# Retention followed by two feed-forward blocks: all eight pairs of the first product of token chunks 2 and 3 by Strassen's scheme

## The chip, the core and the metric

The kernel runs on one core of a Trainium2 chip. Its engines are TensorE (PE in the profile; its weight loads have a row of their own, PEld), VectorE (DVE), ScalarE (ACT), GpSimd (POOL) and SyncE (SP), which here only issues DMAs. The metric is the device time of one execution in microseconds (us), as the median of several runs. The profile describes one execution.

## What is computed

```python
# retention: q, k, v of (2, 8, 768, 64); gamma and scale per head
for t in range(S):
    state = gamma * state + einsum('bhd,bhe->bhde', k[:, :, t], v[:, :, t])
    y[:, :, t] = scale * einsum('bhd,bhde->bhe', q[:, :, t], state)
x = y as (1536 tokens, 512)
# block 1: w_in (512, 2048), w_out (2048, 512)
h = x @ w_in
x = softplus(h) @ w_out
# block 2: w_in (512, 2048), w_out (2048, 512)
h = x @ w_in
out = (h * clip(h + 3, 0, 6) / 6) @ w_out
```

Some inputs arrive as float64, and the kernel makes float32 words of them itself (`Words.made`: raw bits to `cv` on ACT and DVE).

## The kernel before

**Arithmetic.** Every float32 operand of a product is split in two parts, high and low, each of which TensorE takes in one pass. A product is three passes: high x high, high x low, low x high. The split is always the same two instructions (`parted`): ACT copies the operand into the high part, DVE subtracts that from the operand for the low part.

**Tiles.** The 1536 tokens are three chunks of 512 columns (chunk 0, 1, 2 in the code; the words of the change call them 1, 2, 3). The hidden 2048 columns are 16 tiles f of 128. G1(c, f) is the first product of block 1 for one chunk and one tile: 12 matmuls of 128x512 into one bank. G2(c, f) is the second product: 12 matmuls of 128x512 into four accumulating banks. In between stands the softplus of one tile (`softplus`): DVE e, ACT e, DVE g, ACT hi, DVE lo.

**Strassen's scheme.** Two neighbouring tiles f are a pair p, eight in all. For chunks 1 and 2 together, a pair's first product is a 2x2 by 2x2 block product (two halves of the 512 input rows, two tiles, two chunks), and the scheme with seven half-products in place of eight makes it. The half-products are L1 to L7 (P1 to P7 in `early_step`), each 6 matmuls of 128x512. Seven of them give both tiles for both chunks, which plain G1 makes in 8 times 6 matmuls. The tokens' operands of the half-products are the tiles `xl`, one for each of the seven; four of them need sums that `early_operands` makes in place in the chunks' tiles `x` (t1 to t4). The weights' operands (`we`) come from the words of `w_in`, which are written to DRAM once (`words_in`), fetched again a pair at a time (`wf`) and summed by DVE (`sums`) in `early_in` and `forms`. The banks of a pair are combined in `early_step`: ACT `basel` copies L1's bank, L2 adds to that bank and ACT copies it to `g`; DVE then makes `partl`, `totall`, two `hs` and a `g`. Chunk 1's results go on as `g`; chunk 2's (`hs`) go to DRAM (`stash_h`) and come back later.

**Which pairs.** `PLAIN = 1`: pair 7 (tiles 14 and 15) is made by plain G1 for chunks 1 and 2, pairs 0 to 6 by the scheme.

**Order.** A planner (`Plan.run`) fixes each engine's order when the program is built: every task has an engine, a cost, what it waits for and a due time. The due times come from the list `pe`, which writes TensorE's order out: retention's blocks (`Tk`, `Tq`, `SS`, `DD`, `II`, `CC` for two blocks of 128 tokens at a time) stand in the gaps between the G1 and G2 of chunk 0, then come the half-products with G2 of chunk 1 between them (`behind`), then G2 of chunk 2, then block 2. Every engine runs its list in order; a waiting instruction holds up all behind it.

**What stays where.** A tile of weights has one of 20 slots `w`. The `w_out` tiles 8 to 15 are written to DRAM (`parts_out`) after chunk 0 and read back for chunks 1 and 2, except those of pair 7, which stay for chunk 1.

Of the kernel before, what the change touches and what calls it, by code (L numbers as in the profile page):

```python
# [18 lines left out]
P = 128  # L19
# [126 lines left out]
def kernel(ctx, tc, q, k, v, w1_in, w1_out, w2_in, w2_out, table, out):  # L146
# [19 lines left out]
    PLAIN = 1  # L166
# [80 lines left out]
    for name, n, shape, dtype in (("sums", 1, [P, 4, CH // 2], F32), ("wf", 1, [P, 2, CH], F32), ("xl", 7, [P, 2, 2, CH], F32R), ("hs", 3, [P, CH], F32), ("g2", 5, [P, CH], F32), ("hi2", 7, [P, CH], F32R), ("lo2", 7, [P, CH], F32R),  # L247
                                  ("basel", 1, [P, CH], F32), ("partl", 2, [P, CH], F32), ("totall", 1, [P, CH], F32), ("xf", 7, [P, 2, 2, QT], F32R), ("keep", START + 2, [P, CH], F32), ("tf0", 2, [P, 2, QT], F32), ("tf1", 2, [P, 2, QT], F32), ("tf2", 2, [P, 2, QT], F32),
# [25 lines left out]
    ORDER[2] = [f for pair in zip(range(KEPT), range(KEPT, NF)) for f in pair]  # L274
    FIRSTS = [c * NF + f for c in range(NC) for f in ORDER[min(c, 1)][:2 * PLAIN if c else NF]]
# [21 lines left out]
    for i, s in enumerate(FIRSTS):  # L297
        if s == 2 * NF + ORDER[1][0]:
            pe += [x for n in sorted(gaps) for x in gaps[n]] + [("L1", 0), ("L2", 0)]
            gaps.clear()  # L300
        for key in [("G1", s)] + ([("G2", FIRSTS[i - LAG])] if i >= LAG and FIRSTS[i - LAG] < 2 * NF else []):
# [5 lines left out]
    behind = [("G2", s) for s in FIRSTS[-LAG:] if s < 2 * NF]  # L307
# [30 lines left out]
    def dve(n):  # L338
        return (n + 151) / 960 - 0.05
# [65 lines left out]
    def weight(o, f, number):  # L405
# [28 lines left out]
        if not o and f // 2 in PAIRS:  # L434
            home = homes["in", f] = kept(f"words_in{f}", CH)
            T["S", key] = nc.add("SP", 0.45, lambda: nc.sync.dma_start(out=home, in_=x.w().bitcast(F32)), [t5], use, give=[x.cv_k] + made, load=0.8)
        elif o and f >= KEPT:
# [3 lines left out]
            for c_of in range(1 + (f in ORDER[1][:2 * PLAIN]), 3):  # L441
# [38 lines left out]
    def early_in(p):  # L480
        at = due["L1", p] - (12 if p else 18.0)
# [19 lines left out]
    def forms(m, p, words_of, t, words_k, at):  # L501
# [26 lines left out]
        for n, (source, cols, after, give) in enumerate((  # L528
# [3 lines left out]
                (lambda: pair(2), whole, [s3, s4], [sums[1]]))):  # L532
# [702 lines left out]
```

## Time and profile before

| | |
|---|---|
| time, median of 3 runs | 564.74 us (564.32 to 564.96) |
| the profiled execution's own time | 564.72 us |
| its span in the profile | 562.8 us |
| PE busy, 3685 matmuls | 553.3 us, 98% of the span |
| DVE, ACT busy | 440.5 us (78%), 367.1 us (65%) |
| from 150 us to 300 us: DVE busy by stretches of 50 us | 41.8, 44.4, 49.4 us |

The span runs from the first to the last instruction; the own time of the execution adds 1.9 us around it. Retention and chunk 0 fill the first 150 us, the half-products of chunks 1 and 2 with the G2 of chunk 1 the time to about 260 us, G2 of chunk 2 the time to some 300 us, block 2 the rest.

### The profile page before, as it was taken

To read this page: it belongs to the slowest core of one execution; us is meant where nothing else is said; L and a number is where in the kernel's file an instruction comes from. 1 tells how busy PE (TensorE), PEld (TensorE's weight loads), DVE (VectorE), ACT (ScalarE), POOL (GpSimd) and SP (SyncE) were. 2 spreads that over 40 slices of the span, in tenths; PEclk is the share of its full clock that TensorE was granted. 3 is DMA by queue.
4 is the path that set the end of the run, shared out by engine and by line. 5 is a ranking of instruction groups with operands and counts; after the bars stand their busy time and mean duration, and the time that the engine had idled before them with its cause. 6 is when DMAs were issued, how large, how long until landed. Compare 5 with 4: busy or idle time off the path is not lost.

```text
span 562.8 us, 9577 instructions
## 1 busy us (share of the span) xinstructions
PE 553.3 (98%) x3685; PEld 473.3 (84%) x3685; DVE 440.5 (78%) x778; ACT 367.1 (65%) x600; POOL 5.8 (1%) x13
## 2 busy tenths in 40 slices
PE   8899999999999999999999999999999999999996
PEld 6687788888788888888888999988998889988895
DVE  5999998889799778999998775837887897854443
ACT  4697999997774536687968734448778775432220
POOL 0000000000000000000000000000000000000000
PEclk9999999999999999999999999999999999999999
DMA  9997999994422216988907522243755752236003
GB/s 208 286 238 257 285 294 285 324 236 158 151 75 76 75 62 205 323 305 281 358 21 279 187 75 76 82 180 112 229 183 186 272 177 76 75 106 231 1 0 113
DMA packets 80829, 100.51 MB, mean 179 GB/s; under 512 B 41360, under 2 KB 58000, under 8 KB 80784
## 3 DMA queue, kind: packets, MB, share of 16 engines
q1 hardware_dynamic: 79776, 98.45, 54.3%
q0 software_dynamic: 720, 1.31, 1.3%
q8 instruction: 29, 0.48, 0.3%
q10 hardware_dynamic: 288, 0.14, 0.1%
q14 instruction: 16, 0.13, 0.1%
HBM read 74.98 MB, written 23.59 MB: 175 GB/s over the span
## 4 chain that ended last, share of the span: by engine, by line
PE 82%; DVE 5%; ACT 5%; DMA 5%; issue 1%; DVEq 0%; ACTq 0%; SPq 0%
PE banks L45 82%; DMA raw<-in_moe_w_in_dram 3%; ACT cv L45 2%; DMA raw<-in_moe_w_out_dram 1%; DVE g L45 1%; DVE cv L45 1%; DVE raw L45 1%; DVE lo L45 1%; DMA stash_out<-raw 1%; ACT hi L45 1%; ACT raw L45 0%; DVE qT L45 0%; DMA out_dram<-ob 0%; ACT between L45 0%; ACT w L45 0%
## 5 line engine op out<-in xcount | busy, mean ns | idle before, releaser
L45 PE MATMUL banks<-w,parts 128*128 128x512 f32 x579 | 136.7, 390 | 0.0
L45 PEld LDWEIGHTS banks<-w,parts 128*128 128x128 f32 x579 | 108.0, 188 | 21.3
L45 PE MATMUL banks<-hi,w 128*128 128x512 f32 x384 | 124.8, 393 | 0.0
L45 PE MATMUL banks<-xf,w 128*128 128x384 f32 x672 | 123.2, 337 | 0.4 <-DVE c L45 0.4
L45 PEld LDWEIGHTS banks<-xf,w 128*128 128x128 f32 x672 | 118.3, 188 | 3.4 <-DVE c L45 0.7
L45 PEld LDWEIGHTS banks<-hi,w 128*128 128x128 f32 x384 | 72.1, 188 | 15.0
L45 PE MATMUL banks<-xl,w 128*128 128x512 f32 x342 | 81.0, 391 | 0.2
L45 PEld LDWEIGHTS banks<-xl,w 128*128 128x128 f32 x342 | 63.7, 188 | 14.1 <-DVE hs L45 0.5
L45 PE MATMUL banks<-lo,w 128*128 128x512 f32 x192 | 75.1, 391 | 0.2 <-DVE lo L45 0.2
L45 ACT ACTIVATE e<-c,three 128x384 f32<-128x384 f32 (+1 forms) x32 | 24.6, 770 | 47.0 <-DVE c L45 46.5
L45 ACT ACTIVATE cv<-raw,half 128x512 uint32<-128x512 uint32 x64 | 48.6, 761 | 7.5 <-DMA raw<-in_moe_w_out_dram 3.7
L45 ACT ACTIVATE cv<-raw 128x512 f16<-128x512 int32 x64 | 50.0, 788 | 1.2
L45 DVE SCALAR_TENSOR_TENSOR cv<-raw,cv 128x512 uint32<-128x512 uint32 x64 | 44.1, 690 | 1.4
L45 PE MATMUL banks<-x_hi,w 128*128 128x512 f32 x128 | 42.5, 399 | 1.0 <-ACT x_hi L45 1.0
L45 PEld LDWEIGHTS banks<-lo,w 128*128 128x128 f32 x192 | 36.1, 188 | 7.9 <-DVE lo L45 0.9
L45 DVE TENSOR_SCALAR raw<-raw 128x512 f32<-128x512 f32 x76 | 32.3, 430 | 11.4 <-ACT raw L45 10.5
L45 ACT ACTIVATE hi<-g 128x512 fp32r<-128x512 f32 x48 | 29.9, 626 | 16.7 <-PE banks L45 10.1
L45 DVE TENSOR_TENSOR lo<-g,hi 128x512 fp32r<-128x512 f32 x48 | 33.0, 688 | 8.0 <-ACT hi L45 7.8
L45 ACT ACTIVATE parts<-c 128x768 fp32r<-128x768 f32 x32 | 26.9, 842 | 18.6 <-DVE c L45 18.6
L45 DVE TENSOR_TENSOR parts<-c,parts 128x768 fp32r<-128x768 f32 x32 | 30.6, 957 | 10.2 <-ACT parts L45 9.9
L45 ACT ACTIVATE e<-e 128x512 f32<-128x512 f32 x48 | 29.7, 624 | 9.3 <-DVE e L45 9.2
L45 ACT ACTIVATE raw<-raw 128x512 f32<-128x512 f32 x52 | 34.4, 668 | 0.7
(95 smaller groups left out, 653.5 us busy)
## 6 DMA issues: line engine op xcount, KB each, us to landing
raw<-in_moe_w_in_dram SPq DMA_DIRECT2D x32, 512.0 KB, 5.6
raw<-in_moe_w_out_dram SPq DMA_DIRECT2D x32, 512.0 KB, 5.7
w<-stash_out SPq DMA_DIRECT2D x32, 512.0 KB, 5.4
stash_out<-raw SPq DMA_DIRECT2D x16, 512.0 KB, 3.4
w<-parts_out SPq DMA_DIRECT2D x14, 512.0 KB, 5.4
parts_out<-w SPq DMA_DIRECT2D x8, 512.0 KB, 4.3
stash_h<-hs SPq DMA_DIRECT2D x16, 256.0 KB, 2.3
g<-stash_h SPq DMA_DIRECT2D x16, 256.0 KB, 4.6
```

The source lines that it names most:

```text
L45: return self.plan.tc.keep_in_program_order(getattr(self.engine, op)(*args, **kwargs))
```

## The change

Pair 7 is made by the scheme as well, so that `gemm1` is left with chunk 0 alone. The pairs come in the order 7, 6, 5, 4 (`LEADS`), then 0, 1, 2, 3 (`REST`). L1 and L2 of the four leads need no sums and no words from DRAM: they take the even tile's own parts (`("w", (0, 0, 2 * p))`) and chunk 1's tokens, and they stand where the plain G1 of pair 7 stood, in the gaps beside retention's last blocks. Since that holds four copies of L1's bank at once, `basel` has 4 slots. The operands `xl` and the sums in `x` are made in two halves of 256 tokens, so that the first half of chunk 2 can be worked on before its last two blocks are there. The `w_out` tiles 8 to 15 all stay for chunk 1 (`STAY`).

```diff
-    PLAIN = 1
+    FRONT = 4
...
-("basel", 1, [P, CH], F32)
+("basel", 4, [P, CH], F32)
...
-    PAIRS = range(NPAIR - PLAIN)
-    ORDER = [list(range(NF)) if c == 0 else list(range(2 * len(PAIRS), NF)) + list(range(2 * len(PAIRS))) for c in range(NC)]
+    PAIRS = [*reversed(range(NPAIR - FRONT, NPAIR)), *range(NPAIR - FRONT)]
+    LEADS, REST = PAIRS[:FRONT], PAIRS[FRONT:]
+    STAY = [2 * p + i for p in LEADS[:FRONT] for i in range(2)]
...
-    FIRSTS = [c * NF + f for c in range(NC) for f in ORDER[min(c, 1)][:2 * PLAIN if c else NF]]
+    FIRSTS = list(range(NF))
...
+    behind = [("G2", s) for s in FIRSTS[-LAG:]] + [("G2", NF + f) for f in ORDER[1][:2 * FRONT]]
+    for i, p in enumerate(LEADS):
+        for block in [("L1", p), ("L2", p)], behind[:1]:
+            pe += gaps.pop(n, [])
+            n += 1
+            pe += block
+        behind = behind[1:]
...
     for p in PAIRS:
-        if behind and p == 0:
-            pe += [("L1", p), behind[0], ("L2", p), behind[1]] + [(name, p) for name in ("L6", "L7", "L5", "L4", "L3")]
-        else:
-            pe += [(name, p) for name in (("L1", "L6", "L2", "L7") if p else ("L6", "L7"))] + behind[:1] + [(name, p) for name in ("L5", "L4", "L3")] + behind[1:]
-        behind = [("G2", NF + 2 * p + i) for i in range(2)]
+        pe += [(name, p) for name in (("L6", "L7") if p in LEADS else ("L1", "L6", "L2", "L7"))] + behind[:1] + [(name, p) for name in ("L5", "L4", "L3")]
+        behind = behind[1:]
+        if p in REST:
+            if p != REST[0]:
+                pe += behind[:1]
+                behind = behind[1:]
+            behind += [("G2", NF + 2 * p + i) for i in range(2)]
...
+            if n == 0 and not m and p in LEADS:
+                continue
...
     def early_operands():
...
+        n = CH // 2
+        for y in range(2):
+            cols = slice(y * n, (y + 1) * n)
+            have = [[t for u in range(c * START + 2 * y, c * START + 2 * y + 2) for t in ready["x", u]] for c in (1, 2)]
...
+            w_key, x_key = ("w", (0, 0, 2 * p)) if n == 0 and p in LEADS else ("we", p, n), ("xl", name)
```

Three places in the built order carry the prediction. Names in the rows: `xl` are the seven token operands, `w` a slot of weights, `hi` and `lo` the parts of a G2, `qT`, `kT` and `st` are retention's.

**TensorE, the leads' L1 and L2.** Before, plain G1 of pair 7 for chunk 1 (two operands `xl` in a row are one G1) stands ahead of retention's scores and its `vs,k` block, rows 407 to 423 of PE:

```order
L45 MATMUL banks<-xl_1664,w_1536 128x512 x6
L45 MATMUL banks<-xl_1668,w_1536 128x512 x6
L45 MATMUL banks<-qT_0_161,kT_0_159 64x64 x16
L45 MATMUL banks<-qT_1_162,kT_1_160 64x64 x16
```

Of the change, L1 and L2 of the leads in the same place and just behind it, rows 407 to 427 (lead 7 is `w_1540`, lead 6 `w_1336`; the rows of a G2 between are left out):

```order
L45 MATMUL banks<-xl_1641,w_1540 128x512 x6
L45 MATMUL banks<-qT_0_163,kT_0_161 64x64 x16
L45 MATMUL banks<-qT_1_164,kT_1_162 64x64 x16
L45 MATMUL banks<-xl_1644,w_1540 128x512 x6
...
L45 MATMUL banks<-xl_1641,w_1336 128x512 x6
L45 MATMUL banks<-hi_95,w_1551 128x512
L45 MATMUL banks<-lo_96,w_1551 128x512
L45 MATMUL banks<-hi_95,w_1551 128x512
L45 MATMUL banks<-xl_1644,w_1336 128x512 x6
```

L1 and L2 of a lead now have something between them: retention's scores for lead 7, three matmuls of a G2 for lead 6; retention's last `CC` stands there for lead 5, a whole G2 for lead 4.

**TensorE, the rest of the leads.** Rows 501 to 514 of the change, behind L6, L7 of lead 7 and a G2. In this order they are L5, L4, L3 of lead 7, then L6, L7, L5 of lead 6, L6 of lead 5, L4, L3 of lead 6, and L7, L5, L4, L3 of lead 5, of which the last eight rows stand here:

```order
L45 MATMUL banks<-xl_1788,w_1574 128x512 x6
L45 MATMUL banks<-xl_1852,w_1336 128x512 x6
L45 MATMUL banks<-xl_1925,w_1342 128x512 x6
L45 MATMUL banks<-xl_1766,w_79 128x512 x6
L45 MATMUL banks<-xl_1793,w_1540 128x512 x6
L45 MATMUL banks<-xl_1788,w_1336 128x512 x6
L45 MATMUL banks<-xl_1925,w_1381 128x512 x6
L45 MATMUL banks<-xl_1766,w_1540 128x512 x6
L45 MATMUL banks<-hi_94,w_81 128x512
```

Thirteen half-products follow each other here without a G2 between them. Before, the longest run without one is plain G1 of chunk 2 (four times 6 matmuls) and nine half-products, rows 487 to 499.

**VectorE, the operands behind retention's end.** From the first sum that needs chunk 2's last blocks to the low part of L6's operand, before (rows 237 to 245) and of the change (rows 245 to 256):

```order
L45 TENSOR_TENSOR x_183<-x_184,x_183 128x1024
L45 TENSOR_TENSOR xl_1943<-x_184,xl_1943 128x1024
L45 TENSOR_TENSOR xl_1958<-x_184,xl_1958 128x1024
L45 TENSOR_TENSOR x_184<-x_184 128x1024
L45 TENSOR_TENSOR x_184<-x_184,x_183 128x1024
L45 TENSOR_TENSOR sums_1760<-wf_1638 128x256 x2
L45 TENSOR_TENSOR sums_1760<-sums_1760,wf_1638 128x256
L45 TENSOR_TENSOR sums_1760<-wf_1638,sums_1760 128x256
L45 TENSOR_TENSOR xl_1982<-x_184,xl_1982 128x1024
```

```order
L45 TENSOR_TENSOR x_185<-x_186,x_185 128x2x256
L45 TENSOR_TENSOR x_186<-x_186 128x2x256
L45 TENSOR_TENSOR w_87<-sums_1850,w_87 128x512
L45 TENSOR_TENSOR sums_1850<-wf_1757 128x256 x2
L45 TENSOR_TENSOR sums_1850<-sums_1850,wf_1757 128x256
L45 TENSOR_TENSOR sums_1850<-wf_1757,sums_1850 128x256
L45 TENSOR_TENSOR lo_98<-g_93,hi_95 128x512
L45 TENSOR_TENSOR xl_1766<-x_186,xl_1766 128x2x256
L45 TENSOR_TENSOR x_186<-x_186,x_185 128x2x256
L45 TENSOR_TENSOR w_1342<-wf_1757,w_1342 128x256
L45 TENSOR_SCALAR e_90<-g_91 128x512
L45 TENSOR_TENSOR xl_1852<-x_186,xl_1852 128x2x256
```

The operations on tokens are half as long, and the first halves (not shown) stand ahead of these rows. Whole program: PE has 6 matmuls with `xl` fewer (336 for 342), SP 6 reads `w<-parts_out` of 512 KB fewer and 2 more writes of `words_in` and 2 more reads `wf`.

## Rows read from the trace of the kernel before

**Rows 1.** The page's first part: span, busy time and share of each engine.

```profile
span 562.8 us, 9577 instructions
PE 553.3 (98%) x3685; PEld 473.3 (84%) x3685; DVE 440.5 (78%) x778; ACT 367.1 (65%) x600; POOL 5.8 (1%) x13
```

**Rows 2.** Waits of PE from 27 us on: what for, total, times, longest.

```profile
PE banks L45 <- DVE c L45: 0.4, 1, 0.4
PE banks L45 <- DVE lo L45: 0.2, 1, 0.2
```

**Rows 3.** Windows: length, PE (matmuls), PEld, DVE, ACT, POOL, PE clock, DMA, GB/s.

```profile
132.00:140.00 8.00, 8.00 (x139) 6.39 (x137) 7.68 (x16) 5.84 (x11) 0.00 (x0) 1.00 0.43 151
140.00:150.00 10.00, 9.94 (x165) 7.85 (x162) 6.61 (x14) 5.80 (x11) 0.00 (x0) 1.00 0.62 211
170.00:180.00 10.00, 10.00 (x46) 8.28 (x45) 9.76 (x20) 4.79 (x10) 0.00 (x0) 1.00 0.08 28
180.00:190.00 10.00, 10.00 (x46) 8.29 (x45) 6.72 (x13) 4.36 (x8) 0.00 (x0) 1.00 0.31 105
250.00:260.00 10.00, 9.91 (x44) 7.88 (x43) 10.00 (x19) 5.65 (x10) 0.00 (x0) 1.00 1.00 362
```

**Rows 4.** Timeline of PE, 243 to 257 us: start, length, operation, count.

```profile
243.73 5.63 PE L45 MATMUL banks<-xl,w 128*128 128x512 f32 x24
249.20 0.39 PE L45 MATMUL banks<-hi,w 128*128 128x512 f32 x1
251.92 4.62 PE L45 MATMUL banks<-xl,w 128*128 128x512 f32 x18
256.38 0.39 PE L45 MATMUL banks<-hi,w 128*128 128x512 f32 x1
```

**Rows 5.** Timeline of all engines around the first pair's L1 and L2.

```profile
147.33 1.66 PE L45 MATMUL banks<-xl,w 128*128 128x512 f32 x6
148.92 0.69 PE L45 MATMUL banks<-qT,st 64*64 64x64 f32 x32
149.03 0.60 ACT L45 ACTIVATE basel<-banks 128x512 f32<-128x512 f32 x1
149.68 1.66 PE L45 MATMUL banks<-xl,w 128*128 128x512 f32 x6
149.68 1.09 ACT L45 ACTIVATE x<-banks 128x512 f32<-128x512 f32 x2
150.80 1.23 DVE L45 TENSOR_TENSOR x<-x,x 128x1024 f32<-128x1024 f32 x1 [1.02 <-ACT x L45]
151.17 0.39 PE L45 MATMUL banks<-hi,w 128*128 128x512 f32 x1
```

**Rows 6.** Timeline of PE, retention's scores at 135 us.

```profile
134.97 1.16 PE L45 MATMUL banks<-qT,kT 64*64 64x64 f32 x64
136.07 0.50 PE L45 MATMUL banks<-hi,w 128*128 128x512 f32 x1
```

**Rows 7.** Timeline of DVE, two stretches.

```profile
127.92 2.36 DVE L45 TENSOR_TENSOR xl<-x,xl 128x1024 fp32r<-128x1024 f32 x2
130.19 0.69 DVE L45 TENSOR_TENSOR w<-cv,w 128x512 fp32r<-128x512 f32 x1
...
251.42 0.68 DVE L45 TENSOR_TENSOR totall<-partl,banks 128x512 f32<-128x512 f32 x1
252.02 0.42 DVE L45 TENSOR_SCALAR e<-g 128x512 uint32<-128x512 uint32 x1
252.35 0.68 DVE L45 TENSOR_TENSOR lo<-g,hi 128x512 fp32r<-128x512 f32 x1
...
254.16 0.68 DVE L45 TENSOR_TENSOR hs<-totall,banks 128x512 f32<-128x512 f32 x1
```

**Rows 8.** The page's sixth part: DMA issues, KB each, median us to landing.

```profile
stash_h<-hs SPq DMA_DIRECT2D x16, 256.0 KB, 2.3
wf<-words_in SPq DMA_DIRECT2D x14, 256.0 KB, 3.0
```

More of the change, by code (lines that the diff above doesn't have):

```diff
@@ L247 @@
     for name, n, shape, dtype in (("sums", 1, [P, 4, CH // 2], F32), ("wf", 1, [P, 2, CH], F32), ("xl", 7, [P, 2, 2, CH], F32R), ("hs", 3, [P, CH], F32), ("g2", 5, [P, CH], F32), ("hi2", 7, [P, CH], F32R), ("lo2", 7, [P, CH], F32R),
-                                  ("basel", 1, [P, CH], F32), ("partl", 2, [P, CH], F32), ("totall", 1, [P, CH], F32), ("xf", 7, [P, 2, 2, QT], F32R), ("keep", START + 2, [P, CH], F32), ("tf0", 2, [P, 2, QT], F32), ("tf1", 2, [P, 2, QT], F32), ("tf2", 2, [P, 2, QT], F32),
+                                  ("basel", 4, [P, CH], F32), ("partl", 2, [P, CH], F32), ("totall", 1, [P, CH], F32), ("xf", 7, [P, 2, 2, QT], F32R), ("keep", START + 2, [P, CH], F32), ("tf0", 2, [P, 2, QT], F32), ("tf1", 2, [P, 2, QT], F32), ("tf2", 2, [P, 2, QT], F32),
                                   ("base", 1, [P, QT], F32), ("part", 2, [P, QT], F32), ("total", 1, [P, QT], F32),
@@ L297 @@
     for i, s in enumerate(FIRSTS):
[L298 to L301, printed above, removed]
+        for key in [("G1", s)] + ([("G2", FIRSTS[i - LAG])] if i >= LAG else []):
             pe += gaps.pop(n, [])
@@ L433, in weight @@
         T["W", key] = [a, b]
-        if not o and f // 2 in PAIRS:
+        if not o:
             home = homes["in", f] = kept(f"words_in{f}", CH)
@@ L440, in weight @@
                        give=[("w", key)], load=1.6)
-            for c_of in range(1 + (f in ORDER[1][:2 * PLAIN]), 3):
+            for c_of in range(1 + (f in STAY), 3):
                 back(("wl", c_of, f), home, c, due["G2", c_of * NF + f] - 8.0, 2.0)
@@ L480, in early_in @@
     def early_in(p):
-        at = due["L1", p] - (12 if p else 18.0)
+        at = due["L6" if p in LEADS else "L1", p] - (12 if p in REST else 18.0)
         wf = "wf", ("wf", p)
@@ L912, in early_operands @@
     def early_operands():
-        v = lambda j, c: x_of("", 1 + c)[:, 2 * j:2 * j + 2]
-        have = [[t for u in range(c * START, (c + 1) * START) for t in ready["x", u]] for c in (1, 2)]
-        when = {name: due[LONE[name], 0] for name in PRODUCTS}
-        if PLAIN:
-            when["P1"] = when["P2"] = due["G1", NF + ORDER[1][0]]
-            when["B12"] = when["P3"] = due["G1", 2 * NF + ORDER[1][0]]
-        def form(name, source, after, at):
-            key = "xl", name
-            T["xl", name] = list(parted(2 * CH, lambda i: at_slot(key)[:, i], source, after, at - (6.0 if name in BY_DMA else 2.5), [], [("xl", key)], name in BY_DMA))
-            return T["xl", name]
@@ L925, in less @@
-        def less(to, a, b, after, at):
-            return [nc.add("DVE", dve(2 * CH), lambda: nc.vector.tensor_tensor(to, a, b, ALU.subtract), after, at)]
-        p1 = form("P1", lambda: v(0, 0), have[0], when["P1"])
-        p2 = form("P2", lambda: v(1, 0), have[0], when["P2"])
-        t1 = less(v(0, 0), v(0, 1), v(0, 0), have[1] + p1, when["P6"] - 5.1)
-        more = form("B12", lambda: v(0, 1), have[1], when["B12"]) if PLAIN else []
-        t3 = less(v(0, 1), v(1, 1), v(0, 1), t1 + more, when["P6"] - 5.0)
@@ L933, in early_operands @@
-        p3 = form("P3", lambda: v(1, 1), have[1], when["P3"] if PLAIN else when["P6"] - 2.4)
-        t2 = less(v(1, 1), v(1, 1), v(0, 0), t3 + p3, when["P6"] - 3.7)
-        t4 = less(v(1, 0), v(1, 0), v(1, 1), t2 + p2, when["P4"] - 3.7)
-        for name, source, after in (("P6", v(1, 1), t2), ("P7", v(0, 1), t3), ("P5", v(0, 0), t1), ("P4", v(1, 0), t4)):
-            form(name, lambda source=source: source, after, when[name])
+        when = {name: due[LONE[name], PAIRS[0]] for name in PRODUCTS}
```

29 lines of the change are left out of this document (24 added, 5 removed).

## Prediction

> **What bounds the kernel now.** I read the page's busy times first, then the waits of PE, then windows over the part that changes. PE is busy in 553.3 of 562.8 us, DVE in 78% [rows 1]. From 27 us on PE's recorded waits come to 0.6 us [rows 2], so between the start and the last output the time is the sum of what PE issues: whoever wants to shorten it must take matmuls away, and every wait that a change gives PE is paid in full. The windows say what that costs the others. In the half-products DVE is nearly as full as PE: 9.76 of 10 us at 170 us and 10.00 of 10 at 250 us, and still PE loses nothing in the first of these and about a third of a microsecond in the second [rows 3]. PE's clock is granted in full (1.00) in every window shown, which is the level of 2.4 GHz.
>
> **What is removed.** Pair 7 for chunks 1 and 2 is four G1 of 12 matmuls, 48; by the scheme it is 7 times 6, 42. Six matmuls of 128x512 go. What one is worth is the distance from start to start, not its length in the row, since they overlap: 24 of them begin at 243.73 and the next thing at 249.20, so 228 ns each, and the 12 of the G2 behind them take 2.72 us, 227 ns each [rows 4]. Six are **1.37 us**. A half-product is 1.37 us, a G2 2.72 us.
>
> By the Trainium skill, "TensorE: Matmul & The Clock Gate", section "Wait — 56ns, not 53.3ns?", matmuls in a row at 2.4 GHz start N / 2.4 GHz plus some 2.5 ns apart, 215.7 ns at N = 512; six would be an estimated 1.29 us and the forecast 0.08 us later. The rows have 228 ns, and with a new weight load for every matmul the row decides.
>
> **What is added on PE: waits inside the leads.** L2 adds to the bank that ACT must first copy (`basel`). In the first pair of before, L1 starts at 147.33 and its six slots are over at about 148.8, where retention's last block starts at 148.92; ACT copies from 149.03 for 0.60 us, and L2 starts at 149.68 [rows 5]. L2 can thus begin some 0.86 us after L1's last slot, if ACT is free. What now stands between:
> - lead 7: retention's scores, 1.10 us [rows 6]. Covered, if ACT isn't late; ACT has four halves of `xl` for two wholes ahead of it, a little more work, so 0 to 0.4 us. I take 0.
> - lead 6: three matmuls of a G2, 0.68 us. 0.18 us short. I take 0.18, with 0 to 0.6.
> - lead 5: the block that covered it before, with the same small loss. 0 net.
> - lead 4: a whole G2. 0.
>
> **What is moved: the operands behind retention's end.** The sums that need all of chunk 2 can start when ACT has copied the last two blocks, 150.80 us, where DVE had idled 1.02 us for it [rows 5]. Up to there PE's order has the same work in it as before, in other places, so I keep 150.80. DVE has the first halves to do ahead of that (four sums and five low parts at 0.60 us), and three weight operations of lead 7 in place of pair 0's; that is some 4.2 us more between 136 and 150 us, against 0.3 us idle in the window from 132 and 3.4 us in that from 140 [rows 3]. DVE comes up to 0.6 us late. Then come the thirteen operations shown in the order, seven of them at 0.60 us a slot and six short ones at 0.34 us (two steps of the timeline: `totall` to `e` 0.60, `e` to `lo` 0.33 [rows 7]), in all 6.2 us. L6's operand for lead 7 is ready at 157.0 to 157.7 us. PE asks for it after L2 of lead 5 (from 149.68 to 151.17), G2, L1 of lead 4, G2 and L2: 151.17 + 2.72 + 1.37 + 2.72 + 1.37 = 159.4 us. It has 1.5 us in hand, so **0**; without that cover each microsecond DVE is late costs one. Some of the DVE work is the price of cutting in halves: 1024 columns go in 1.13 us a slot (two from 127.92 to 130.19), twice 512 in 1.20 us [rows 7], and ten instructions more come to 0.7 us. The Trainium skill, "Perfetto Trace Analysis", section "Optimizing Scalar/DVE Operations", has larger operations pay where an engine is saturated and breaking up pay where it isn't but makes others wait; by it the cut would cost its 0.7 us where DVE is full, and the windows have it less than full at just this place.
>
> **The rest of the leads.** From L6 of lead 7 to the G2 behind L3 of lead 5 PE has 15 half-products and one G2: 15 x 1.37 + 2.72 = 23.3 us. DVE must finish the `hs` that L3 of lead 5 waits for (it adds to that bank) before 21.9 us of it are over, and can begin on the first `partl` some 1.6 us in (a half-product, and 0.25 us until its result is seen, as from 148.8 to the copy at 149.03 [rows 5]). In the order DVE has 23 operations of 512 columns and 12 short ones between, 23 x 0.60 + 12 x 0.34 = 17.9 us in 20.3 us. Going through them one by one, with each that reads a bank not before that half-product is over, I find DVE waiting for PE about 1.6 us in all, and each `totall` and `hs` that PE waits for ready 0.4 to 0.6 us ahead. So **0**, by a small margin. The upper end: if every one of the 35 ran at its full length and a handover, 0.68 us [rows 7] and 0.05 us (149.63 to 149.68 [rows 5]) in place of 0.60, DVE would need 35 x 0.13 = 4.6 us more and PE would wait 2.2 us. Another way to lose it: the second half of lead 4's words is queued on SP behind a store of `hs` (`wf`, `stash_h`, `wf`), which waits for DVE's `hs` behind L5 of lead 7, at about 167.3 us (159.4 + 3 x 1.37 + 2.72, and the operation); with 3.0 us to landing [rows 8] the words are there at 170.5 and DVE's turn for the sums comes at some 171.7 us. 1 us in hand, and up to 1 us if it lands late.
>
> **At no cost:** two more stores and reads of words and six reads of 512 KB fewer, since no wait of PE is on a transfer [rows 2]; the pairs' new order behind 183 us, where DVE had 3.3 us idle in ten [rows 3]; G2 of the last pair at the end of chunk 2. One loss of before could go: at 251.92 eighteen half-product matmuls take 4.46 us, 0.36 more than at 228 ns, because `hs` starts on DVE only at 254.16 [rows 4, 7]. DVE's queue there is another one afterwards, with some 4 us more work in all; I leave it at 0, with -0.36 and +0.4 as bounds.
>
> **Sum.** The profiled execution took 564.72 us, 0.02 under the median. 564.72 - 1.37 + 0.18 = **563.5 us**. 0.2% of this kernel is 1.13 us, about what its measurement can tell from no change, so the forecast of -1.2 us lies hardly beyond it.
>
> **The rivals.**
> - *Eaten up.* The matmuls go, and small waits for `basel`, `totall` and `hs` take 0.3 us or more of it back, since they all have half a microsecond or less in hand: lead 7's 0.4, lead 6's 0.6, SP's 1 us are its bounds. 563.7 to 565.4, about 564.4. For it: the thin margins. Against it: the planner's list has the three matmuls of G2 put where a wait is, and a DVE at 9.76 of 10 us cost PE nothing at 170 us [rows 3].
> - *More than the matmuls.* The 0.36 us at 254 us goes too: 563.1 or, without lead 6's wait, 562.9. For it: DVE reaches this place with its pairs in another order. Against it: DVE has more work, not less.
> - *DVE becomes the bound, slower.* In the 23 us without G2 there is nothing on PE that doesn't want DVE's answer. If DVE's share goes over 21.9 us there, PE waits for all that is over; at full lengths 2.2 us, which makes 565.7 us. It decides against the change from a loss of 1.2 us on. For it: 13 of the 35 operations read a bank that was just finished. Against it: nine half-products in a row ran at the same share of DVE before, at 170 us, without loss [rows 3].
> - That the change doesn't do what it says is excluded by the order: 336 matmuls with `xl` for 342.
>
> **Chances.** Forecast 0.50 (563.2 to 563.7), eaten up 0.28, more 0.10, DVE the bound 0.12. The line of 0.2% is 563.6 us: nine tenths of the forecast's cases and all of "more" are faster, with 0.55 in sum; the rest of the forecast and nearly all of "eaten up" within it, 0.33; DVE the bound, 0.12. Range: 562.8 to 565.4, which leaves out the upper part of the last case and the ends of the others.
>
> **What the profile after would show.** PE busy shorter by 1.4 us and 3679 matmuls. L2 of lead 6 begins 0.1 to 0.3 us after the third G2 matmul's slot, with `basel` as releaser; a larger gap there is "eaten up". No idle PE before the first L6 at about 159 us; a gap there would say that the halves came late. Between 159 and 183 us DVE over 9 of 10 and PE without gaps; gaps of PE on `hs`, `totall` or `partl` there are the slower rival, and a DVE wait on `wf` at 171 us the SP one. A PE gap near 253 us on `hs` gone or still there tells "more". I would be wrong above all if a place outside the half-products moved: the one PE wait on `c` in block 2 [rows 2] should stay as it is.

## The result and the profile after

The change makes the kernel slower: 569.97 us (median of 6 runs, 568.86 to 571.89) against 564.53 us for the kernel before beside it (563.93 to 565.15), a ratio of 1.0100 (95% interval 1.0081 to 1.0119), 5.4 us. The forecast was 563.5 us in a range from 562.8 to 565.4. The profiled execution took 568.86 us, the shortest of the six, with a span of 567.0 us, 4.2 us more than before [rows 1].

The matmuls did go, as the page's first part shows, which answers to [rows 1]:

```profile
span 567.0 us, 9582 instructions
PE 553.7 (98%) x3679; PEld 473.8 (84%) x3679; DVE 443.9 (78%) x797; ACT 365.4 (64%) x604; POOL 5.8 (1%) x13
```

There are 3679 matmuls for 3685, but the busy time of PE has not fallen by 1.4 us: it has risen from 553.3 to 553.7. A busy time that grows while work is taken away points to the clock. The waits of PE (what for, total, times, longest) name the rest; these two rows are new beside [rows 2] (0.4 us of the 2.3 stand in the first 27 us, as before):

```profile
PE banks L45 <- DVE seen L45: 2.3, 2, 2.0
...
PE banks L45 <- ACT basel L45: 2.0, 1, 2.0
```

The timeline of PE (start, length, operation, count, in brackets the idle time ahead of it and its releaser) shows where they are; its rows from 147 us on answer to [rows 5], the last two to [rows 4]:

```profile
141.70 0.39 PE L45 MATMUL banks<-hi,w 128*128 128x512 f32 x1
142.10 1.66 PE L45 MATMUL banks<-xl,w 128*128 128x512 f32 x6
...
147.30 1.66 PE L45 MATMUL banks<-xl,w 128*128 128x512 f32 x6
150.92 0.69 PE L45 MATMUL banks<-qT,st 64*64 64x64 f32 x32 [1.95 <-DVE seen L45]
153.65 2.93 PE L45 MATMUL banks<-xl,w 128*128 128x512 f32 x6 [2.04 <-ACT basel L45]
156.38 0.63 PE L45 MATMUL banks<-hi,w 128*128 128x512 f32 x1
156.80 0.63 PE L45 MATMUL banks<-lo,w 128*128 128x512 f32 x1
...
254.28 4.27 PE L45 MATMUL banks<-xl,w 128*128 128x512 f32 x18
258.39 0.39 PE L45 MATMUL banks<-hi,w 128*128 128x512 f32 x1
```

L1 of lead 5 starts at 147.30, where the first pair's L1 started before (147.33). Then retention's last `CC` block starts at 150.92 instead of 148.92, and L2 of lead 5 at 153.65 instead of 149.68: 2.0 and another 2.0 us. Behind that, six matmuls take 2.73 us, from 153.65 to 156.38, where they took 1.49 [rows 5], and the next two starts are 0.42 us apart. The windows (length, then busy time and instructions of PE, PEld, DVE, ACT and POOL, PE clock, DMA share, GB/s) say why:

```profile
147.60:153.70 6.10, 2.11 (x39) 1.36 (x37) 4.63 (x11) 4.56 (x11) 0.00 (x0) 0.87 0.24 86
153.70:159.00 5.30, 5.30 (x13) 4.13 (x14) 4.84 (x11) 4.30 (x8) 0.00 (x0) 0.51 0.02 3
159.00:169.00 10.00, 10.00 (x45) 8.13 (x44) 8.16 (x15) 8.12 (x15) 0.00 (x0) 1.00 0.20 53
```

After an idle stretch (2.11 us of work in 6.10 us) the granted clock is 0.51 for 5.3 us, the level of 1.2 GHz, and PE is counted as busy throughout.

Matching every matmul's start with the same one of before gives a balance. At 136.9 us, ahead of every changed place that counts, the execution is 0.34 us ahead; leads 7 and 6 cost 0.30; the wait for `seen` 2.04; the wait for `basel` 1.97; the lower clock 2.43, so that PE is 6.40 us behind at 158.94 us. From there to 261.11 us (256.38 before) it makes up 1.67 us: 1.37 for the six matmuls, and 0.30 of the loss near 254 us. That leaves 4.73 us, and 4.2 at the end of the span, since the wait for `c` that the kernel before has in block 2 [rows 2] is not there after the change. The gain is there, and the losses (6.74 us) are four times as large.

**Who was late.** The chain of waits that ended last (start, length, what) passes through this place like this:

```profile
142.10 4.38 PE banks L45 x47
...
146.50 0.64 ACT xl L45
...
147.17 0.69 DVE xl L45
...
150.79 0.08 DVE seen L45
...
150.92 0.51 PE banks L45 x16
...
151.45 0.63 ACT xl L45
152.08 0.52 ACT hi L45
152.59 0.52 ACT e L45
153.12 0.49 ACT basel L45
...
153.65 4.63 PE banks L45 x10
```

Read it twice over: PE, then ACT's `xl`, then others, then PE. An `xl` of ACT is a copy from the tile `x` to the tile `xl`, and both lie in SBUF. Nothing of PE goes into it, and yet it follows PE twice. The view of the tile `xl` on ACT has it in two lines:

```profile
L45 ACT ACTIVATE xl<-x x2: 629/629/629, 146.5 to 151.4; 128x512 fp32r<-128x512 f32 x2
...
  PE banks L45: 5.3, 2
who waited for it (us, times):
  DVE xl L45: 3.3, 1
```

ACT stood idle for 5.3 us ahead of these two copies, until PE had finished something. VectorE waited 3.3 us for the first of them, to make the low part, and `seen` stands further back in its queue. The program's order has this wait too, in rows 208 and 213 of ACT (here with the semaphores that each instruction waits for):

```
208 L45 ACTIVATE xl_5_1852<-x_2_186 128x2x256 [waits DMAHW4_49,DMAHW5_49,DVE_49,PE_49]
...
213 L45 ACTIVATE xl_6_1925<-x_1_185 128x2x256 [waits DVE_49,PE_49]
214 L45 ACTIVATE hi_0_94<-g_1_92 128x512 [waits DVE_49]
215 L45 ACTIVATE e_0_89<-e_0_89 128x512 [waits DVE_49]
216 L45 ACTIVATE basel_2_1957<-banks_64 128x512 [waits PE_49]
```

`xl_5` and `xl_6` are the operands of P6 and P4, 8 KB in each partition. By the addresses of the built program `xl_5` lies where the tiles `vs` and `k` of retention's last two blocks lie, and `xl_6` where `qT`, `vs` and `pw` of these blocks lie; when they are placed, no other hole of 8 KB is left. PE has to finish the blocks that read those tiles before ACT may write the first half of an operand there. So the first half, which the change put ahead of retention's end, waits for retention's end, and since ACT takes its list in order, `basel`, `hi` and `e` wait behind it. Before, every `xl` of these operands stood behind retention's end anyway, and the same memory wait cost nothing.

### The profile page after: what moved, and what is told of

Same layout as the page of the kernel before. It is cut to its first block, busy times and chain, and to the rows that moved or that the text cites. A ratio compares the mean times of both kernels' runs of the same rounds, so it can differ in the third digit from the quotient of the medians.

```text
span 567.0 us, 9582 instructions
## 1 busy us (share of the span) xinstructions
PE 553.7 (98%) x3679; PEld 473.8 (84%) x3679; DVE 443.9 (78%) x797; ACT 365.4 (64%) x604; POOL 5.8 (1%) x13
## 4 chain that ended last, share of the span: by engine, by line
PE 95%; DVE 1%; ACT 1%; DMA 1%; issue 0%; DVEq 0%
PE banks L45 95%; DMA k<-in_k_dram 0%; DVE qT L45 0%; ACT cv L45 0%; DMA out_dram<-ob 0%; DVE ob L45 0%; ACT xl L45 0%; ACT x_hi L45 0%; DVE w L45 0%; DVE sums L45 0%; DVE xl L45 0%; ACT raw L45 0%; DVE x L45 0%; DVE g L45 0%; ACT e L45 0%
```

## The experiments

These theories stand against each other. **A**: ACT's queue is blocked by memory that retention still reads, and the lower clock follows from PE's idle time. **B**: VectorE has no room around retention's end, so what is moved only waits elsewhere. **C**: the clock fell by itself. **D** and **F** speak of block 2, where some of the loss is to be found in some executions; a rival **H** to B comes with e13. The variants change the place of single instructions: the planner still plans the change's order, but a task with `behind` is written out only after the task named there. The kernel before ran beside them each time, with medians of 563.99 to 564.44 us.

### e1: the two blocked first halves behind retention's end

```diff
                 T["xl", name] = T.get(("xl", name), []) + made
+                if y == 0 and name in ('P6', 'P4'):
+                    for t in made:
+                        t.behind = ready["x", 3 * START - 1][0]
```

> The change with one thing moved: the first halves of xl for P6 and P4 (a copy on ScalarE and a subtraction on VectorE each) stand behind the two copies of retention's last results instead of ahead of them; everything else keeps its place in every queue. Theory A (blocked queue): in the changed kernel these two copies write memory that retention's last blocks still read, ScalarE waits in them for TensorE, and VectorE (seen) and ScalarE (basel) come late for TensorE, 1.95 and 2.04 us, and the clock of 0.51 behind it costs 2.4 us more. Then both waits go, the clock stays at 1.00, and the time is that of the kernel before less the six matmuls (1.37 us) and the 0.3 us that went at 254 us: 564.5 - 1.7 = 562.8 us, 562.3 to 563.6. Rival B (too much work): the four basel copies and the halves are simply more than ScalarE and VectorE can do beside retention's end; then some 4 us of waits stay wherever the copies stand, and the time is 566 to 570 us. Rival C (clock by itself): the clock falls at this place whether TensorE waits or not; then about 2.4 us stay, 565.2 us.

Measured: 565.15 us (564.31 to 567.0, 12 runs), ratio 1.0020 (1.0006 to 1.0035): 0.7 us above the kernel before beside it, where the change had 5.4. The median lies above A's range and happens to be the number of C (565.2), so the traces have to decide. The timeline of PE:

```profile
149.10 0.69 PE L45 MATMUL banks<-qT,st 64*64 64x64 f32 x32
149.85 1.66 PE L45 MATMUL banks<-xl,w 128*128 128x512 f32 x6
...
155.43 0.39 PE L45 MATMUL banks<-hi,w 128*128 128x512 f32 x1
156.84 0.50 PE L45 MATMUL banks<-lo,w 128*128 128x512 f32 x1 [1.02 <-DVE lo L45]
```

The block and L2 start 0.18 us later than before [rows 5], not 2 and 4 us, and the window where the clock was 0.51 now has it in full:

```profile
153.70:159.00 5.30, 4.28 (x19) 3.23 (x18) 5.20 (x12) 4.55 (x9) 0.00 (x0) 1.00 0.19 51
```

So A holds, for both waits and for the clock, and C's low clock isn't there: nothing else was moved. But a new wait of 1.2 us (156.84 less 155.43, less 0.23 for the start between) stands at 156.84, for a `lo` of VectorE, whose window has it busy in 5.20 of 5.30 us.

### e2: only P4's first half

```diff
+                if y == 0 and name in ('P4',):
+                    for t in made:
+                        t.behind = ready["x", 3 * START - 1][0]
```

> As the run before it, but only the first half of xl for P4 is moved behind the copies of retention's last results; that for P6 stays ahead. Theory A: the first wait (TensorE for seen, 1.95 us, by way of P6) stays, the second (for basel, 2.04 us, by way of P4) goes. If the clock falls from the sum of both waits, one of them alone may leave it at 1.00: 562.8 + 2.0 = 564.8 us; if it falls all the same, 567.2 us. Rival B (too much work): both waits stay, about 570 us.

570.13 us (569.2 to 570.64, 4 runs), ratio 1.0106 (1.0087 to 1.0126). Of the waits of PE, the first stays and the second shrinks:

```profile
PE banks L45 <- DVE seen L45: 2.4, 2, 2.0
...
PE banks L45 <- ACT basel L45: 0.4, 1, 0.4
```

Each blocked copy thus has a wait of its own: P6's that for `seen`, P4's that for `basel`. At 256 us this kernel is 2.07 us behind before, for 4.73 of the change; what the profiled execution loses again after that comes from block 2 (waits of 2.2 us for `base` there). The median is thus the 570 us that the rival had forecast, though the second wait did not stay; for the other executions the loss in block 2 is not shown.

### e3 and e8: idle time put into the kernel before

`basel` of the first pair is copied nine times (e3) or five times (e8, with `else 5`) in the kernel before, so that L2 waits; nothing else is changed.

```diff
-        a1 = nc.add("ACT", ACP, lambda: nc.scalar.activation(at_slot(base), bank(1), AF.Copy), [p1], ...
+        a1 = nc.add("ACT", ACP, lambda: [nc.scalar.activation(at_slot(base), bank(1), AF.Copy) for _ in range(1 if p else 9)], [p1], ...
```

> The kernel before with one suspected cost put in by itself: in the first pair ScalarE makes the copy basel nine times in place of once (the same values), so that L2, for which TensorE then waits, is held some 8 x 0.52 = 4.2 us at the same place as in the change, 149.7 us. Theory A (idle TensorE loses its clock): the clock falls to about 0.5 behind it as in the changed kernel, and the loss is 4.2 us and 2.4 us, 571.1 us. Rival C (the clock falls for another reason that belongs to the change): clock 1.00, 568.7 us.

> The kernel before with the copy basel of the first pair made five times in place of once (the same values): eight more copies held L2 by 5.0 us in the third run, so four should hold it by 2.5 us. If the clock falls only behind a longer idle time, the loss is 2.5 us, 566.9 us; if it falls behind this one too, it is 2.5 + 2.5 us, 569.4 us. In the second run a wait of 2.2 us and one of 0.7 us close behind were followed by a stretch at half clock of only five matmuls, so I expect something between, nearer to 567.5 us.

e3: 571.87 us (571.12 to 572.7, 4 runs), ratio 1.0139 (1.0120 to 1.0159). e8: 568.66 us (566.91 to 569.02, 4 runs), ratio 1.0069 (1.0049 to 1.0090), dearer than the 567.5 expected. The windows of e3, the idle stretch and what follows it:

```profile
149.20:154.50 5.30, 0.28 (x20) 0.14 (x12) 0.44 (x1) 5.05 (x10) 0.00 (x0) 0.82 0.00 0
154.50:159.70 5.20, 5.13 (x13) 4.02 (x14) 4.17 (x4) 5.14 (x9) 0.00 (x0) 0.52 0.01 3
```

The second of them in the kernel before:

```profile
154.50:159.70 5.20, 5.20 (x25) 4.30 (x24) 5.13 (x8) 5.14 (x8) 0.00 (x0) 1.00 0.00 0
```

And of e8:

```profile
150.50:153.20 2.70, 0.22 (x16) 0.08 (x7) 0.38 (x1) 2.57 (x6) 0.00 (x0) 1.00 0.00 0
153.20:156.60 3.40, 3.31 (x9) 2.65 (x10) 2.35 (x3) 3.37 (x6) 0.00 (x0) 0.60 0.02 5
```

The kernel before has its clock in full here; with 5.1 us of waiting put in, it has the change's picture, half the clock for 5.2 us, and eleven starts, nearly all some 427 ns apart, cost 2.3 us more. With 2.6 us of waiting, eight starts cost 1.55 us more. C falls: idle time alone brings the lower clock, in a kernel without any other edit, and e1 has the edit without the idle time and without the lower clock.

### e4: the operands whole again, the rest of the change kept

```diff
-        n = CH // 2
-        for y in range(2):
-            cols = slice(y * n, (y + 1) * n)
-            have = [[t for u in range(c * START + 2 * y, c * START + 2 * y + 2) for t in ready["x", u]] for c in (1, 2)]
+        n = CH
+        for y in range(1, 2):
+            cols = slice(0, CH)
+            have = [[t for u in range(c * START, (c + 1) * START) for t in ready["x", u]] for c in (1, 2)]
```

> The change with one part undone: the operands xl and the sums in x are made whole, behind retention's end, as before, not in token halves. No copy then stands ahead of retention's end in ScalarE's queue, so by theory A the waits for seen and basel at 149 to 154 us go and the clock stays at 1.00. What it costs is the work that had been moved ahead: 9 operations of 0.60 us, 5.4 us less 0.7 us for the cutting. L6 of the first pair is then ready at about 159.3 us where TensorE asks at 159.4, and VectorE has 4.7 us more in the stretch to 183 us, where it had 2.4 us to spare: a loss of 0 to 3 us, 562.8 to 566 us, about 564.5. Rival B (too much work for ScalarE and VectorE at 149 us): waits of TensorE for basel stay at 2 us each, 566 us or more.

568.94 us (567.88 to 569.73, 4 runs), ratio 1.0081 (1.0058 to 1.0105), above the 566 us that was A's upper end. The waits at 149 to 154 us and the lower clock are gone, since no copy stands ahead of retention's end; but all the operands' work now comes behind it, and PE waits later, above all here:

```profile
171.25 2.08 PE L45 MATMUL banks<-xl,w 128*128 128x512 f32 x8 [1.44 <-DVE totall L45]
```

Smaller gaps stand at 165, 181 and 247 us. At 260.0 us this execution is 3.62 us behind before, of which 1.17 stood there already at 138 us. So the halves have a purpose: they let VectorE begin ahead of retention's end, and without them its load behind it costs PE more than the six matmuls give. That is B, in another place than the rival in the expectation had it (`basel` at 149 us).

### e5 and e9: other halves moved, and `lo` ahead

e5 leaves P6 and P4 where they can be written without a memory wait and moves P5's and P7's first halves behind P6's second half. e9 also moves P5's first low part behind the `lo` that PE waited for, and two weight operations of pair 6 behind P5's second low part.

```diff
+    for t, task in ((T["xl", "P7"][0], T["xl", "P6"][2]), (T["xl", "P7"][1], T["xl", "P6"][3]), (T["xl", "P5"][0], T["xl", "P6"][2]), (T["xl", "P5"][1], T["xl", "P7"][3])):
+        t.behind = task
```

> The change with the first halves of xl for P5 and P7 moved behind the second half of P6, in place of those for P6 and P4 (these stay ahead of retention's end, as in the change). Five slots of xl are all that can be written while retention's last blocks are read; now P6 and P4 have two that nobody reads any more, and P5 and P7 get theirs when retention is over. Theory A (blocked queue): no copy on ScalarE waits for TensorE, and VectorE has the low parts of P6 and P4 done ahead of retention's end, so the wait that the first of these runs still had (TensorE for lo at 155 to 157 us, 1.18 us) goes as well: 565.15 - 1.2 = 564.0 us, 563.0 to 564.6. Rival B (too much work for VectorE behind retention's end): the 1.2 us come back as a wait for the operand of L6 or L7 of the first pair, at 158 to 161 us, and the time stays at 565.2 us.

> The fifth run (first halves of P5 and P7 behind) with three operations of VectorE moved behind the low part lo that TensorE still waited for there, 1.23 us at 161.6 us: the first half of P5's low part and two sums of weights that are wanted only at some 168 us. Theory A: nothing waits any more up to 256 us, where the fifth run was 0.9 us ahead of the kernel before: now 2.1 us ahead. What is lost in block 2 (1 to 2 us in the fifth run) stays: 565.97 - 1.2 = 564.7 us, 563.9 to 565.4. Rival B (VectorE is simply full): the wait comes back at the next operand, L5 or L4 of the first pair at 164 to 166 us, and the time stays at 566 us.

e5: 565.97 us (564.94 to 567.39, 9 runs), ratio 1.0031 (1.0019 to 1.0043). e9: 565.4 us (564.04 to 566.49, 12 runs), ratio 1.0018 (1.0007 to 1.0030). Both medians lie above what A alone would give (564.0 and 564.7).

What e5 shows of A is in ACT's timeline:

```profile
142.64 0.63 ACT L46 ACTIVATE xl<-x 128x512 fp32r<-128x512 f32 x1 [0.33 <-DVE x L46]
146.43 0.62 ACT L46 ACTIVATE xl<-x 128x512 fp32r<-128x512 f32 x1
```

These are the same two copies as in the change, in the same place ahead of retention's last block (148.46 us here), but into memory that by the program's addresses nobody reads any more, and without a semaphore of PE. ACT doesn't wait for PE ahead of them, and the waits of PE at 149 to 154 us are gone. So it is the memory that held them in the change, and not their place in the queue; of the amount of work e16 speaks below.

In e5 PE waits for `lo` in another place:

```profile
161.59 0.39 PE L46 MATMUL banks<-hi,w 128*128 128x512 f32 x1
163.05 0.50 PE L46 MATMUL banks<-lo,w 128*128 128x512 f32 x1 [1.07 <-DVE lo L46]
```

In e9 this wait is gone, and one of the same size has come:

```profile
167.63 2.74 PE L46 MATMUL banks<-xl,w 128*128 128x512 f32 x11 [1.04 <-DVE totall L46]
```

`lo` at 156.8 in e1, `lo` at 163.1 in e5, `totall` at 167.6 in e9, each about 1.2 us late: a new order moves the wait and leaves its size. That is B.

### e13 to e16: weight sums on GpSimd

Of pair 6 (e13), or of pairs 6 and 5 (e14 on e1's order, e15 on e9's, e16 on the change as it is), the four weight sums go to GpSimd, which does nothing else at this time.

```diff
         def put(n, a, b, op):
-            return lambda: nc.vector.tensor_tensor(total(n), a(), b(), op)
+            return lambda: (nc.gpsimd if not m and p in (6, 5) else nc.vector).tensor_tensor(total(n), a(), b(), op)
```

> The kernel of e1 with the four weight sums of pair 6 (two at 154.64, then 155.31 and 155.76 on VectorE there, 1.6 us in a row) on GpSimd, which is idle from 117 us on. Theory B (VectorE has no room behind retention's end): lo, which began at 156.10 and let TensorE wait 1.2 us, begins 1.2 to 1.6 us earlier, that wait goes, and the profile gains 0.9 to 1.2 us by 256 us: some 1.1 to 1.4 us ahead of the kernel before at 256 us (e1: 0.23), median 563.9 to 564.4 where e1 had 565.15. Its rival H: lo is held by ScalarE's hi, not by VectorE's queue, or GpSimd's adds slow VectorE's; then the wait stays at 0.8 us or more and the median at 565.0 or above. No row so far shows GpSimd adding; if an add takes it 4 times VectorE's 0.42 us, the four are done by about 161.5 us, and their first reader on ScalarE was at 159.77: a wait there of under 2 us, which TensorE sees only at the half-products of pair 6, from about 165 us on.

> As e13, with the four sums of pair 5 (164.24 to 165.7 us in e1) on GpSimd as well. Theory B: nothing more to win in e1's order, since TensorE waits for nothing between 159 and 250 us there: within 0.3 us of e13. If the VectorE queue there was the hidden cause of what e1's median has over its profile, another 0.5 us.

> The kernel of e9 (first halves of the low parts and two weight sums moved so that lo comes in time; TensorE then waits 1.2 us for totall at 166 us) with the sums of pairs 6 and 5 on GpSimd. Theory B: 3.2 us of VectorE's 17 between 152 and 169 us are gone, so the wait for totall goes: 1.2 us ahead of e9 by 256 us, median 564.0 to 564.4 (e9: 565.4). If only order and not the amount of work set those waits, totall stays late: 565.2 to 565.6.

> The change itself with the sums of pairs 6 and 5 on GpSimd; the first halves still stand ahead of retention's end. Theory A (ScalarE's queue is blocked by memory): the waits for seen (2.0) and basel (2.0) and the lower clock behind them stay, since they hang on ScalarE and not on how much VectorE has to do: 569.3 to 570.3. Theory B as the cause of the whole loss: 565 to 566.

e13: 564.94 us (563.84 to 566.35, 12 runs), ratio 1.0013 (1.0002 to 1.0025). e14: 564.92 us (564.39 to 566.77, 12 runs), 1.0015 (1.0003 to 1.0027). e15: 565.54 us (563.81 to 568.45, 12 runs), 1.0023 (1.0007 to 1.0039). e16: 569.82 us (568.72 to 570.96, 4 runs), 1.0105 (1.0083 to 1.0127).

e16 fits A alone: a lighter VectorE doesn't cure the change, and its waits for `seen` and `basel` are 2.0 us each as before. e14 stands with e13, as expected if there was nothing more to win in e1's order. e13 and e15 lie 0.5 and 1.1 us above the ranges of B, in two ways. In e13 the `lo` of 156 us does come in time (it starts at 154.66), but then VectorE slows, as its timeline shows, while GpSimd adds:

```profile
154.66 0.69 DVE L45 TENSOR_TENSOR lo<-g,hi 128x512 fp32r<-128x512 f32 x1
155.26 1.23 DVE L45 TENSOR_TENSOR xl<-x,xl 128x512 fp32r<-128x512 f32 x1
156.53 1.12 DVE L45 TENSOR_TENSOR x<-x,x 128x512 f32<-128x512 f32 x1
157.57 0.96 DVE L45 TENSOR_TENSOR w<-wf,w 128x256 fp32r<-128x256 f32 x1
```

```profile
154.82 1.12 POOL L45 TENSOR_TENSOR sums<-wf 128x256 f32<-128x256 f32 x1 [4.10 <-DVE w L45]
155.91 1.19 POOL L45 TENSOR_TENSOR sums<-sums,wf 128x256 f32<-128x256 f32 x1
157.18 1.07 POOL L45 TENSOR_TENSOR sums<-wf,sums 128x256 f32<-128x256 f32 x1
```

The same forms took 0.68, 0.69 and 0.42 us in e1, so three operations cost 1.52 us more and eat what the sums gave (1.5 us, from 154.64 to 156.10 in e1). Of the rival H, the second half holds. The next `lo` is late instead; of PE:

```profile
163.74 0.50 PE L45 MATMUL banks<-lo,w 128*128 128x512 f32 x1 [1.10 <-DVE lo L45]
```

The Trainium skill, "SBUF — State Buffer", section "SBUF: two separate sides", says that VectorE and GpSimd share one pair of ports as an exclusive lock, taken by VectorE's operations with two SBUF inputs among others, and that whoever starts first holds it for the whole instruction while the other blocks. These rows agree: the operations that grew all read two SBUF tiles, and they grew by 0.55, 0.43 and 0.54 us, where GpSimd's addition had 0.68, 0.57 and 0.68 us left when they began.

In e15 PE's wait for `totall` is down to 0.2 us, so e9's wait was VectorE's load, which is B again. Yet the median does not follow and lies where it was expected if only the order counted (565.2 to 565.6): small gaps of 0.1 to 0.4 us are left at 167, 176 and 252 us, and block 2 takes another 0.5 us in the profiled execution.

### e6, e7, e10, e11, e12: block 2's start

In e5 PE waits 1.1 us for ACT's `base` and 0.4 for `part` where block 2 starts. D had it that ACT converts a tile of weight words first, which waits for a transfer. e6 (on e5) and e7 (on the change) put `base` and `part` ahead of that conversion:

```diff
+    for t in T["late", 5]:
+        t.behind = T["base", 0][t.eng == "DVE"]
```

> The run before it, and at the start of block 2 (some 300 us) ScalarE's copy base and VectorE's part of the first pair stand ahead of the conversion of a tile of weight words that waits for a transfer (five instructions; in the change they stand behind it, in the kernel before ahead of it). Theory D (a second blocked queue): in executions where that transfer lands late TensorE waits 1.7 and 0.6 us there, as the profiles of the second and the fourth run show at 306 to 310 us; this makes the spread of 564.3 to 567.0 us in the first run. Then the upper executions go: a median of 563.2 us (562.4 to 563.9), some 0.8 us below the run without it, and a spread of less than 1.5 us. Rival E: the spread is not from there; then the median and the spread are those of the run before it.

> The changed kernel with nothing but base and part of block 2's first pair moved ahead of that conversion. Theory A: the waits at 149 to 154 us and the low clock behind them (6.4 us) are untouched; theory D takes up to 1.2 us off the median: 568.5 to 570 us. Were the place at 306 us the main cause (rival D alone), the time would fall to 566 us or below.

e6: 567.48 us (565.6 to 568.11, 6 runs), ratio 1.0051 (1.0035 to 1.0068). e7: 571.67 us (571.17 to 574.28, 5 runs), 1.0138 (1.0118 to 1.0158). By their medians both are slower than what they start from, by 1.5 and 1.7 us. The wait for `base` went in e6, and waits of 1.8 us for `c` came: the conversion that was put off is now ahead of the next result. The gain that D had forecast didn't come; whether D names the cause rightly, this edit can't tell, since it only moved the conversion to another place where PE waits for it.

F had it that the words of block 2's third pair come too late. e10 (on e9) and e12 (on the change) fetch them ahead of three tiles of `w_out`, e11 (on e9) ahead of one, and each converts two tiles of `w_out` behind the first results of block 2:

```diff
-        at = due["P1", USED[f // 2]] - (40 - 2.0 * f if f < 2 * MID else 16)
+        at = due["P1", USED[f // 2]] - (14 if f in (3, 4, 5) else 40 - 2.0 * f if f < 2 * MID else 16)
...
+    for f in (4, 5):
+        for t in T["late", f]:
+            t.behind = T["first", 0][t.eng == "DVE"]
```

> The run before it, and block 2's words of its third pair (two tiles of w_in) are fetched ahead of two tiles of w_out, whose conversions stand behind the first pair's base, part, e, c and total in place of ahead of them. Theory F (late words): in the change the tile that was fetched 33 us before block 2's first matmul in the kernel before is fetched 9 us before it, since three slots for words are freed later by a VectorE that has more to do; ScalarE and VectorE then wait for a transfer with block 2's first pair behind them. With the words there early the 1 to 2 us in block 2 go: 564.7 - 1.7 = 563.0 us, 562.0 to 563.6, faster than the kernel before. Rival G: block 2 is slower for another reason (its later pairs); then the time is that of the run without it, 564.7 us.

> As the tenth run, with the smaller exchange: only one tile of w_out (the sixth) is fetched behind the two tiles of w_in, and its conversion and that of the seventh stand behind the first pair's e and total. The second w_in tile is then fetched only some 4 us earlier than in the change. Theory F: between the ninth and the tenth run, 563.0 to 564.5 us, about 563.5. Rival G: 564.7 us.

> The changed kernel with the words' order of the tenth run and nothing else: the waits at 149 to 154 us and the low clock behind them (6.4 us) stay. Theory F: the part that the change loses in block 2 in most executions (none in the profiled one) goes, 1 to 2 us off the 570 to 571.7 us: 568.8 us, 568.2 to 569.6. Rival G: 570 us or above, as in the seventh run.

e10: 573.06 us (572.85 to 574.65, 4 runs), ratio 1.0159 (1.0140 to 1.0178). e11: 573.3 us (572.15 to 574.67, 4 runs), 1.0158 (1.0137 to 1.0179). e12: 578.39 us (576.56 to 579.78, 4 runs), 1.0245 (1.0221 to 1.0270). By their medians all three are 7.7 to 8.4 us slower than what they start from, where F had forecast a gain. The conversions in their new place hold up `c`, so F by itself, words that come earlier and nothing else, stays untested. PE pays for `c` twice, as in the change itself. In e10:

```profile
317.29 2.29 PE L46 MATMUL banks<-xf,w 128*128 128x384 f32 x6 [5.70 <-DVE c L46]
```

```profile
317.30:322.00 4.70, 4.70 (x13) 4.12 (x14) 3.81 (x6) 2.85 (x4) 0.00 (x0) 0.50 0.97 332
```

Another queue, another place in the program, and the same pair: an idle stretch, then half the clock.

## Why the prediction was wrong, step by step

**Six matmuls less are 1.37 us: right.** Between 158.94 and 261.11 us the change makes up 1.67 us, and the part for six starts is 1.37.

**The leads' waits for `basel`: right for 7 and 6, wrong for 5.** Lead 6 was to lose 0.18 us; PE's timeline has the third G2 matmul at 141.70, its slot over at 141.93, and L2 at 142.10, a gap of 0.17. Leads 7 and 6 together cost 0.30. For lead 5 the prediction had "the block that covered it before, with the same small loss. 0 net"; it cost 1.97 us.

**The failed step: "Up to there PE's order has the same work in it as before, in other places, so I keep 150.80."** The end of retention was taken as fixed, and of ACT it was said that four halves in place of two wholes are "a little more work, so 0 to 0.4 us". Their work is small indeed, 0.63 us each. What they wait for was not looked at: two of them write memory that retention's last blocks still read. The step counted the busy time of the moved copies and not when their targets come free. It cost 2.04 us (`seen`), 1.97 us (`basel`) and, through the idle time, 2.43 us of clock. e1 takes these away by moving those two halves alone, e5 by giving them other memory in the same place; e2 shows one wait for each; e3 shows the clock's part.

**That PE's clock would hold was not a step at all.** The prediction says that every wait "is paid in full". Here 4.0 us of waiting were paid with 6.4 us.

**No loss in the rest of the leads: right in the change, by luck.** Between 159 and 183 us VectorE is busy in 8.7 of 10 us and PE without gaps but for 0.1 us at 168.7, because PE came 6.4 us late and VectorE had worked on. When PE comes in time, VectorE is short of 1.2 us (e1, e5, e9): in e5 and e9 behind L6, within the 2.2 us of the rival "DVE becomes the bound", in e1 ahead of L6, at a `lo` that the prediction counts among the operations before L6's operand but not as one that PE waits for. That the change came late enough to hide this is the reading of these variants; the change itself shows only that nothing was lost. The other way to lose it, words that land late, isn't seen: VectorE has no wait for `wf` between 159 and 185 us.

**The 0.36 us near 254 us: gone.** This is the rival "more than the matmuls". The eighteen take 4.11 us of after's timeline (254.28 to 258.39), 228 ns each, where they took 4.46 [rows 4].

**"I would be wrong above all if a place outside the half-products moved."** That is what happened, with retention's last block. None of the rivals named it. The place it was thought of for, the wait for `c` in block 2 that "should stay as it is", is not in the profile after.

**The cut in halves.** By the Trainium skill, "Perfetto Trace Analysis", section "Optimizing Scalar/DVE Operations", breaking up pays where an engine isn't full but makes others wait. e4 agrees: with whole operands PE waits behind retention's end, and the median is 3.8 us above that of e1, which has the halves. The halves are wrong only where a half has no memory to go to.

**What stays open.** With A's loss taken away (e1, e13, e14) the medians are 0.7 to 1.0 us above the kernel before beside them, while a sum of the steps shown (1.67 gained, 0.30 and 1.2 lost) would leave them 0.2 below. Some of it lies outside the span: the time less the span is 2.18 us in e1 (median) and 1.95 in e13 and e14, where the kernel before has 1.80; why is not known. And single profiles differ by more than is sought: from 256 us to the end, which the change was not meant to touch, they lose between -0.5 us (the change) and +2.8 us (e2) against the profile of before, and up to 137 us, where nothing that counts was changed, they differ by 1.9 us among themselves (0.77 ahead in e5, 1.17 behind in e4). Block 2's start takes some of the gain in some executions; which transfer or conversion decides it was not settled. No version here beats the kernel before.

## What to carry to other kernels

Moving an instruction ahead needs two things ready: its input, and the memory that it writes. Look in the order of the changed program for a copy between SBUF tiles that waits for TensorE; with tiles placed automatically, that is a wait for a tile's last reader, and in a queue that runs in order it holds up everything behind it. Where TensorE is the bound, price a wait of a few microseconds at more than itself, since half the clock may follow, and a helper engine that is nearly full gives a moved piece of work back as a wait elsewhere.

## What the runs showed of the hardware that was not expected

- **Idle time lowers the clock soon.** Behind a wait of 2.6 us (e8) the granted clock was 0.60 over the next 3.4 us and cost 1.55 us; behind two of 2.0 us with a small block between them (the change) 0.51 and 2.43 us; behind 5.1 us (e3) 0.52 and 2.3 us; behind 5.7 us (e10) 0.50. Behind waits of 1.0 to 1.4 us (e1, e4, e5, e9, e13) it stayed at 1.00. The Trainium skill, "TensorE: Matmul & The Clock Gate", section "HAM oscillation — how this bites in real kernels", describes waits on transfers after which TensorE starts cold again; here the waits were on other engines' queues, and the clock fell as well.
- **GpSimd's additions slow VectorE.** An addition of 128x256 took GpSimd 0.72 to 0.74 us where VectorE stood idle (e14, e16) and 1.1 to 1.2 us beside VectorE's operations, where VectorE took 0.42, and VectorE's operations on two SBUF tiles beside it took 0.96 to 1.23 us for 0.42 to 0.69 (e13). In e14 it went the other way: two of GpSimd's additions took 3.77 us together where VectorE had a full row of such operations, each at its 0.68 us.
